# A tile of 56 words behind the constants of a convolution and feed-forward kernel on one core

## Chip, core and metric

The kernel runs on one core of one Trainium2 chip. The metric is the device time of one execution in microseconds, lower is better. Engines are named as in the profile: PE is TensorE's matmul, PEld its weight load, DVE VectorE, ACT ScalarE, POOL GpSimd, SP SyncE.

## What is computed

A long convolution by FFT, gated by its input, and then a feed-forward layer with silu on every token. B = 2, S = 12,480, D = 128, d_ff = 2,048.

```python
h_filt = (np.maximum(pos_emb @ w1, 0.0) @ w2) * np.exp(-0.01 * pos)[:, None]
u = x * v
y = irfft(rfft(u, 2 * S) * rfft(h_filt, 2 * S))[:, :S]
t = (x * y).reshape(B * S, D)
h = t @ w_in
out = (h / (1.0 + np.exp(-h))) @ w_out
```

## The kernel before, in words

The transform of 2 x 98 x 64 points is done as matmuls with tables of sines in two stages. Five stretches follow each other in the program, and the order in each is written out by hand (strings of letters, and tables of offsets).

1. To some 125 us: products x * v, stage A of batch 0 (L224, into X), the filter's first layers (zp, z) and their stage A (aph, into Xha and Xhb). The feed-forward weights, which arrive as 64-bit floats, are made fp32 beside it.
2. To some 300 us, a loop of 49 pairs of frequencies for batch 0: filter spectrum (hp, sp, hab), forward transform (up, L437), complex product (at, bt), inverse transform (wp, L437), store (ws, L492). The table fb is loaded four pairs ahead, hab is stored to DRAM for batch 1. These matmuls are plain fp32.
3. To some 400 us: stage A of batch 1, and the split of w_in and w_out.
4. To some 957 us: the feed-forward steps of batch 0, and between them, by a table of offsets, the same loop for batch 1 (up and wp, now in fp32r), whose loads and temporaries lie in the buffer slots.
5. To the end: the remaining feed-forward steps alone.

A feed-forward step (L838 to L877) treats 512 tokens and one of 16 blocks of 128 hidden units. Accuracy is kept in fp32r by splitting each operand into a high and a low part and multiplying three times. So a step has three matmuls of 512 columns into hq, with weights from wih and wil and the moving operand ah and al (L845 to L847), and, three steps later, three into op, with weights from woh and wol and the moving operand gh and gl (L875 to L877). The silu (L852), the split into gh and gl (L854 to L857), the last inverse transform of the next tokens (yp, L620) and its split (ah, al, L642) go on beside. There are 49 x 16 = 784 steps; up and wp of batch 1 have 2 x 49 x 6 = 588 matmuls of 256 columns (L437).

Buffers are taken from two sides of SBUF. On the left, from the constants upwards: X, z, and in their turn fb, zt, hab, uw, at, bt, ws, then woh, wol, ring, ah, al, gh, gl, ot, g and the split operands of up and wp (xs, fw, iv, vs with h and l). On the right, from the top downwards: the staged x and v, the weights' temporaries, Xha, Xhb, then slots, wih, wil and spare. In the built program the first left buffer behind the constants, X, starts at byte 20,480 of each partition; woh at 120,832, wol at 129,024, ah at 141,312, gh at 149,504: all left buffers from X on start at multiples of 512. On the right wih starts at 187,360, wil at 195,552, slots at 203,744: 32 bytes short of a multiple of 512.

Of the kernel before, what the change touches and what calls it, by code (L numbers as in the profile page):

```python
# [10 lines left out]
F32 = mybir.dt.float32  # L11
# [83 lines left out]
def kernel(  # L95
# [20 lines left out]
    def pool(name, **kw):  # L116
        kw.setdefault("bufs", 1)
        return tc.alloc_tile_pool(name=name, reuse_waits="tile", **kw)
# [8 lines left out]
    const = pool("const")  # L127
# [4 lines left out]
    win_sb = const.tile([R, 128], F32, name="win_sb")  # L132
    w1_sb = const.tile([128, 128], F32, name="w1_sb")
    w2_sb = const.tile([128, D], F32, name="w2_sb")

    def weights(wp, src, nm, bufs, dst):

# [834 lines left out]
```

## Time and profile before

| | us |
|---|---|
| median of 3 runs (lowest, highest) | 1614.35 (1613.84, 1619.06) |
| profiled execution | 1615.36 |
| its span, first to last instruction | 1613.6 |
| busy: PE, DVE, ACT, POOL | 1582.2, 1234.4, 1058.5, 566.3 |

TensorE's granted clock is 0.993 of full speed over the span. Busy times of matmuls are of limited use, since they are pipelined: one of 512 columns is shown with about 0.39 us, and the next starts 0.23 us after it. Start times in the timeline are therefore read beside the means. The chain of waits follows the work that ended last back to the start, and the table by stages tells which engine has no idle time where.

### The profile page before, as it was taken

How to read it: one execution, taken by the hardware profiler on the slowest of the kernel's cores; microseconds unless marked ns; L12 is line 12 of the kernel's file. 1: busy time of each engine (PE TensorE's matmuls, PEld its weight loads, DVE VectorE, ACT ScalarE, POOL GpSimd, SP SyncE). 2: the span in 40 equal slices, each digit the busy share in tenths (PEclk: the TensorE clock that was granted, in tenths of full speed). 3: DMA queues.
4: the chain of work that ended last, by engine and by line, in shares of the span. 5: the costliest groups of instructions: out<-in, count | busy, mean ns of one | idle time of the engine just before them, and what ended most of it. 6: DMA issues, size and time to landing. Idle time of an engine off the chain costs nothing.

```text
span 1613.6 us, 29344 instructions
## 1 busy us (share of the span) xinstructions
PE 1582.2 (98%) x10904; PEld 1316.2 (82%) x10904; DVE 1234.4 (77%) x1983; ACT 1058.5 (66%) x1929; POOL 566.3 (35%) x564
## 2 busy tenths in 40 slices
PE   7799999899999999999999999999999999999999
PEld 7797877688888888888888888888888888888887
DVE  5946888755688988889988887777777777777776
ACT  4548888687777777777777765555555555555554
POOL 4627779532266666666666630000000000000000
PEclk9899999899999999999999999999999999999999
DMA  8817888834355454455545521111111211111100
GB/s 256 244 62 210 235 248 250 235 115 119 91 145 149 130 140 129 132 140 137 149 132 141 145 78 47 48 33 45 51 32 45 66 33 45 51 32 45 51 28 14
DMA packets 125767, 180.75 MB, mean 112 GB/s; under 512 B 10528, under 2 KB 72360, under 8 KB 125624
## 3 DMA queue, kind: packets, MB, share of 16 engines
q1 hardware_dynamic: 85560, 141.14, 31.7%
q10 hardware_dynamic: 40064, 37.73, 8.1%
q8 instruction: 86, 1.41, 0.4%
q14 instruction: 57, 0.47, 0.1%
HBM read 125.42 MB, written 53.41 MB: 111 GB/s over the span
## 4 chain that ended last, share of the span: by engine, by line
PE 92%; DMA 4%; DVE 2%; POOL 1%; issue 1%; ACT 0%; SPq 0%; ACTq 0%; POOLq 0%; DVEq 0%
PE op L875 12%; PE hq L846 11%; PE hq L845 11%; PE op L877 11%; PE hq L847 11%; PE op L876 11%; PE yp L620 6%; PE wp L437 4%; PE up L437 4%; PE ap L224 3%; PE sp L316 2%; PE aph L358 2%; PE hp L297 2%; DMA xs<-in_x_dram 2%; DMA fb<-in_fb_dram 1%
## 5 line engine op out<-in xcount | busy, mean ns | idle before, releaser
L852 ACT ACTIVATE g<-hq 128x512 f32<-128x512 f32 x424 | 253.8, 599 | 238.8 <-PE hq L847 227.9
L857 DVE TENSOR_TENSOR gl<-g,gh 128x512 fp32r<-128x512 f32 x424 | 293.6, 693 | 99.1 <-ACT gh L856 66.4
L875 PE MATMUL op<-gh,woh 128*128 128x512 f32 (+1 forms) x784 | 313.8, 400 | 0.0
L845 PE MATMUL hq<-ah,wih 128*128 128x512 f32 (+1 forms) x784 | 309.2, 394 | 0.9 <-DVE gl L857 0.8
L846 PE MATMUL hq<-al,wih 128*128 128x512 f32 (+1 forms) x784 | 309.7, 395 | 0.0
L877 PE MATMUL op<-gh,wol 128*128 128x512 f32 (+1 forms) x784 | 308.7, 394 | 0.0
L847 PE MATMUL hq<-ah,wil 128*128 128x512 f32 (+1 forms) x784 | 308.2, 393 | 0.0
L876 PE MATMUL op<-gl,woh 128*128 128x512 f32 (+1 forms) x784 | 305.7, 390 | 0.0
L852 ACT ACTIVATE hq<-hq 128x512 f32<-128x512 f32 (+1 forms) x360 | 206.7, 577 | 101.6 <-PE hq L847 85.0
L857 DVE TENSOR_TENSOR gl<-hq,gh 128x512 fp32r<-128x512 f32 (+1 forms) x360 | 244.7, 684 | 33.3 <-ACT gh L856 23.3
L854 DVE CAST gh<-hq 128x512 fp32r<-128x512 f32 (+1 forms) x270 | 183.3, 679 | 54.8 <-ACT hq L852 53.0
L854 DVE CAST gh<-g 128x512 fp32r<-128x512 f32 x318 | 135.7, 427 | 66.4 <-ACT g L852 65.2
L847 PEld LDWEIGHTS hq<-ah,wil 128*128 128x128 f32 x784 | 146.9, 187 | 35.5
L846 PEld LDWEIGHTS hq<-al,wih 128*128 128x128 f32 x784 | 146.9, 187 | 34.8 <-DVE al L643 0.2
L875 PEld LDWEIGHTS op<-gh,woh 128*128 128x128 f32 x784 | 147.6, 188 | 33.5
L845 PEld LDWEIGHTS hq<-ah,wih 128*128 128x128 f32 x784 | 147.4, 188 | 32.9 <-DVE gl L857 1.6
L877 PEld LDWEIGHTS op<-gh,wol 128*128 128x128 f32 x784 | 147.1, 188 | 31.4
L876 PEld LDWEIGHTS op<-gl,woh 128*128 128x128 f32 x784 | 147.7, 188 | 27.5 <-DVE gl L857 0.3
L230 ACT COPY X<-ap 64x392 f32<-64x392 f32 x208 | 100.0, 481 | 39.4 <-PE ap L224 36.8
L620 PEld LDWEIGHTS yp<-fai_sb,slots 98*64 98x64 f32 x2048 | 89.3, 138 | 19.2 <-issue 18.7
L620 PE MATMUL yp<-fai_sb,slots 98*64 98x97 f32 (+1 forms) x2048 | 99.3, 251 | 0.0
L475 DVE TENSOR_TENSOR at<-at,bt 128x768 f32<-128x768 f32 x49 | 72.5, 1479 | 19.5 <-POOL bt L469 19.0
(1059 smaller groups left out, 2400.5 us busy)
## 6 DMA issues: line engine op xcount, KB each, us to landing
slots<-hs SPq DMA_DIRECT2D x98, 256.0 KB
slots<-wd SPq DMA_DIRECT2D x48, 490.0 KB
hs<-hab SPq DMA_DIRECT2D x49, 256.0 KB
wd<-ws SPq DMA_DIRECT2D x49, 256.0 KB
slots<-in_fb_dram SPq DMA_DIRECT2D x49, 256.0 KB
wd<-slots ACTq DMA_DIRECT2D x49, 256.0 KB
out_dram<-ot ACTq DMA_DIRECT2D x48, 256.0 KB
fb<-in_fb_dram ACTq DMA_DIRECT2D x45, 256.0 KB
```

The costliest lines, as they stand in the source:

```text
L230: nc.scalar.copy(out=o, in_=src[:, k0:k1])
L437: nc.tensor.matmul(out[:, k].rearrange("p i d -> p (i d)"), f[:, k], a[:, k], start=(i == 0), stop=(i == len(passes) - 1),)
L620: nc.tensor.matmul(yp[h : h + 64, o : o + ws[t]], wt[:, c, t * D + h : t * D + h + 64], fai_sb[:, c, 0 : ws[t]], start=(c == 0), stop=(c = ...
L845: nc.tensor.matmul(hp[:, 0:w], wih[:, fs], ah[:, 0:w], start=True, stop=False)
L846: nc.tensor.matmul(hp[:, 0:w], wih[:, fs], al[:, 0:w], start=False, stop=False)
L847: nc.tensor.matmul(hp[:, 0:w], wil[:, fs], ah[:, 0:w], start=False, stop=True)
L852: nc.scalar.activation(out=g[:, 0:w], in_=hp[:, 0:w], func=AF.Silu)
L854: nc.vector.tensor_copy(gh[:, 0:w], g[:, 0:w])
L857: nc.vector.tensor_tensor(out=gl[:, 0:w], in0=g[:, 0:w], in1=gh[:, 0:w].bitcast(F32), op=ALU.subtract)
L875: nc.tensor.matmul(o[:, 0:w], woh[:, fs], gh[:, 0:w], start=(f == 0), stop=False)
L876: nc.tensor.matmul(o[:, 0:w], woh[:, fs], gl[:, 0:w], start=False, stop=False)
L877: nc.tensor.matmul(o[:, 0:w], wol[:, fs], gh[:, 0:w], start=False, stop=(f == NF - 1))
```

## The change

One tile is taken from the pool of the constants, behind w2_sb. Nothing writes or reads it. It has 56 words of 4 bytes, so X and every left buffer behind it start 224 bytes higher: X at 20,704, woh at 121,056, gh at 149,728. The constants ahead of it and all buffers on the right stay where they are, and so does PSUM. On every engine and queue the instructions stand in the same order with the same shapes and waits as before.

```diff
     win_sb = const.tile([R, 128], F32, name="win_sb")
     w1_sb = const.tile([128, 128], F32, name="w1_sb")
     w2_sb = const.tile([128, D], F32, name="w2_sb")
+    const.tile([128, 56], F32, name="gap")
```

## Rows read from the trace of the kernel before

**Rows 1.** The page's chain that ended last, by line.

```profile
PE op L875 12%; PE hq L846 11%; PE hq L845 11%; PE op L877 11%; PE hq L847 11%; PE op L876 11%; PE yp L620 6%; PE wp L437 4%; PE up L437 4%; PE ap L224 3%; PE sp L316 2%; PE aph L358 2%; PE hp L297 2%; DMA xs<-in_x_dram 2%; DMA fb<-in_fb_dram 1%
```

**Rows 2.** Stages: length, busy us (count) of PE, PEld, DVE, ACT, POOL; clock, DMA, GB/s.

```profile
125.00:300.00 175.00, 169.23 (x2158) 135.72 (x2159) 142.76 (x204) 143.41 (x258) 141.83 (x148) 1.00 0.84 235
...
400.00:957.00 557.00, 556.96 (x3351) 464.81 (x3350) 484.42 (x744) 420.55 (x800) 336.49 (x347) 1.00 0.50 134
957.00:1613.00 656.00, 652.98 (x3646) 528.37 (x3644) 470.85 (x821) 356.21 (x592) 0.00 (x0) 1.00 0.14 42
```

**Rows 3.** Timeline of TensorE, 1290 to 1297 us: start us, length us, what.

```profile
1290.30 0.39 PE L875 MATMUL op<-gh,woh 128*128 128x512 f32 x1
...
1290.75 0.40 PE L877 MATMUL op<-gh,wol 128*128 128x512 f32 x1
...
1291.45 0.39 PE L847 MATMUL hq<-ah,wil 128*128 128x512 f32 x1
...
1295.84 0.39 PE L875 MATMUL op<-gh,woh 128*128 128x512 f32 x1
```

**Rows 4.** Groups by line and shape, 1289.5 to 1306.5 us: busy us, mean ns | idle.

```profile
L846 PE MATMUL hq<-al,wih 128*128 128x512 f32 x13 | 5.2, 397 | 0.0
L877 PE MATMUL op<-gh,wol 128*128 128x512 f32 x13 | 5.1, 396 | 0.0
L845 PE MATMUL hq<-ah,wih 128*128 128x512 f32 x13 | 5.1, 394 | 0.0
L876 PE MATMUL op<-gl,woh 128*128 128x512 f32 x13 | 5.1, 389 | 0.0
L847 PE MATMUL hq<-ah,wil 128*128 128x512 f32 x12 | 4.7, 393 | 0.0
L875 PE MATMUL op<-gh,woh 128*128 128x512 f32 x12 | 4.7, 389 | 0.0
...
L847 PEld LDWEIGHTS hq<-ah,wil 128*128 128x128 f32 x13 | 2.4, 187 | 0.6
L875 PEld LDWEIGHTS op<-gh,woh 128*128 128x128 f32 x12 | 2.3, 188 | 0.6
```

**Rows 5.** The page's costliest groups: the silu of each step, without and with side work.

```profile
L852 ACT ACTIVATE g<-hq 128x512 f32<-128x512 f32 x424 | 253.8, 599 | 238.8 <-PE hq L847 227.9
...
L852 ACT ACTIVATE hq<-hq 128x512 f32<-128x512 f32 (+1 forms) x360 | 206.7, 577 | 101.6 <-PE hq L847 85.0
```

**Rows 6.** Groups by line and shape, 700 to 712 us, beside batch 1.

```profile
L847 PE MATMUL hq<-ah,wil 128*128 128x512 f32 x8 | 3.2, 396 | 0.0
L845 PE MATMUL hq<-ah,wih 128*128 128x512 f32 x8 | 3.2, 395 | 0.0
L846 PE MATMUL hq<-al,wih 128*128 128x512 f32 x8 | 3.2, 395 | 0.0
L875 PE MATMUL op<-gh,woh 128*128 128x512 f32 x8 | 3.1, 394 | 0.0
L877 PE MATMUL op<-gh,wol 128*128 128x512 f32 x8 | 3.1, 393 | 0.0
L876 PE MATMUL op<-gl,woh 128*128 128x512 f32 x8 | 3.1, 393 | 0.0
```

**Rows 7.** Timeline of TensorE at 707 us, two of six 256-column matmuls.

```profile
707.68 0.28 PE L437 MATMUL up<-xs26l,fw26h 128*128 128x256 f32 x1
707.80 0.28 PE L437 MATMUL up<-xs26h,fw26l 128*128 128x256 f32 x1
```

**Rows 8.** Groups by line and shape, whole span.

```profile
L437 PE MATMUL wp<-at,fb 128*128 128x256 f32 x196 | 51.1, 383 | 3.5 <-POOL at L479 2.6 <-DVE at L479 0.9
...
L491 ACT COPY slots<-wp 128x512 f32<-128x512 f32 x49 | 28.8, 588 | 0.3
L491 ACT COPY ws<-wp 128x512 f32<-128x512 f32 x49 | 28.7, 586 | 14.7 <-ACT hab L318 9.5 <-PE wp L437 3.8 <-issue 1.2
```

**Rows 9.** Chain of waits, 140 to 300 us, by line.

```profile
by line: PE sp L316 21.3%; PE wp L437 19.9%; PE up L437 17.8%; PE hp L297 14.6%; DMA fb<-in_fb_dram 12.5%; DVE at L475 3.6%; issue 2.9%; POOL bt L462 2.3%; POOL bt L469 1.9%; ACT hab L318 0.9%; POOL at L479 0.9%; ACT ws L491 0.4%; ACT uw L4
```

## Prediction

> **What bounds the kernel now.** I read the chain of waits first. By line, the six matmul lines of the feed-forward step (L845 to L847, L875 to L877) hold 67% of it [rows 1]. The busy time by stage says where: in 400 to 957 us TensorE is busy 556.96 of 557 us, in 957 to 1613 us 652.98 of 656 us, while VectorE has 470.85 and ScalarE 356.21 there [rows 2]. So for three quarters of the run a nanosecond per matmul counts at full weight, and a nanosecond on any other engine counts nothing.
>
> Then I looked at those matmuls one by one. Where the side work is over, one step (six matmuls of 512 columns) takes (1295.84 - 1290.30) / 4 = 1.385 us [rows 3]. The six are alike in shape, type and source of the moving operand (left side of SBUF). They are not alike in time. A weight load runs beside the matmul before it, so each matmul is to be read by whose weights load in its shadow. 875, 876 and 847 cover loads of woh, wol and woh, from the left side: 389, 389 and 393 ns. 877, 845 and 846 cover loads of wih, wih and wil, from the right side: 396, 394 and 397 ns. Means 390.3 and 395.7, so **5.3 ns more beside a load from the right** [rows 4]. The start times say the same: 875 to 877 takes 0.45 us for two matmuls, 877 to 847 takes 0.70 us for three [rows 3]. The loads themselves last 187 or 188 ns on both sides [rows 4]. In the built program the left buffers from X on start at multiples of 512 bytes, the right ones 32 bytes short of one. The change puts the left ones at 224 past a multiple of 256, which is where the right ones already stand (256 - 32). That 5.3 ns is what I build on.
>
> **The change part by part.** No instruction, wait or transfer is added, removed or reordered; the unused tile is never written. What differs is the address of every left buffer.
>
> *Weights on the left, steps without side work.* If a load from 224 past a multiple costs what the right side costs now, three matmuls in each of the 424 steps that write g [rows 5] take 5.3 ns more: 424 x 3 x 5.3 = 6.7 us.
>
> *Weights on the left, steps beside batch 1.* Here the six lines are level: 394, 393 and 396 ns beside left loads, 393, 395 and 395 beside right ones [rows 6]. The same classes exist, but the 256-column matmuls between the steps disturb the pattern. If everything goes to the 395.7 of the undisturbed right class, that is 1.4 ns on the six matmuls of 360 steps [rows 5]: 3.0 us. The low end is 0, the high end the whole 5.3 on the three left loads, 5.7 us. I take 3.0, as it starts from this stretch's own rows.
>
> *The 256-column matmuls of up and wp in batch 1.* 2 x 49 x 6 = 588, all with left weights and 0.12 us apart [rows 7]. At 5.3 ns each: 3.1 us; low end 0. I take 3.1, because they have no right neighbours that could have hidden the price already.
>
> *The moving operand.* All 4,704 + 588 of these matmuls stream from the left, so all streams now begin at 224. No row has an fp32r stream from there. Lower bound: a gain, which is the second rival below. Upper bound: another 5.3 ns each, 5,292 x 5.3 = 28.0 us. I take 0, since what the rows vary is the weight side alone, and keep both ends.
>
> *Matmuls in plain fp32 (batch 0, stage A, yp).* They run as two slower passes: 383 ns for 256 columns [rows 8], against 0.28 us for the fp32r form [rows 7]. A stream at that pace has more slack for a late word, so I take 0. At the high end each pays 5.3 ns on 383, 1.4% of the 73.6% of 160 us that sp, wp, up and hp hold on the chain of the batch 0 loop [rows 9]: 1.6 us.
>
> *The other engines.* The same ScalarE eviction takes 588 ns into a right buffer and 586 into a left one [rows 8]. Two nanoseconds per instruction lie under the busy TensorE; if that cover were gone, the 784 silus and 98 evictions like these would cost 1.8 us. VectorE and GpSimd have slack in the same stages [rows 2]. I take 0.
>
> *DMA.* In the batch 0 loop fb, hab and ws are on the left; in batch 1 the same kinds of transfer use the slots on the right. Share of the queues per GB/s: 0.84 / 235 = 0.00357 with left buffers, 0.50 / 134 = 0.00373 with right ones, 4.4% more [rows 2]. The chain of that loop waits for landings of fb for 12.5% of 160 us, 20 us [rows 9]; 4.4% of that is 0.9 us, low end 0. I take 0: the queues go from 0.84 to 0.88 busy and the prefetch is four ahead.
>
> The Trainium skill's page "DMA: Bandwidth & Descriptors" (How a descriptor splits into AXI transactions) speaks against the change: a read that does not start on a multiple of 256 bytes still fetches from the boundary below. By it a 512-byte run of ws would take 23 beats instead of 16, an estimate of 44% on a third of the loop's bytes, so some 15% on those waits, 3 us instead of 0. The 4.4% above, which includes the same 512-byte runs stored from the right, does not bear out so much.
>
> **Sum.** 6.7 + 3.0 + 3.1 = 12.8 us. The profiled execution took 1615.36 us, so 1628.2; the median of the runs, 1614.35, lies 1.0 lower, so **1627 us**. Bounds of this case alone: 1621 (the first term, the others at 0) to 1662 (every high end, 47.8 us).
>
> **The rivals.** *Nothing happens.* The 5.3 ns could belong to where wih and wil lie (at 187 KB of a partition, the left weights at 121 to 137 KB), or to the hq bank they feed, and 224 bytes alter neither. For it: ScalarE is blind to the side within 2 ns [rows 8], and all six lines are level in the stage with side work [rows 6]. Against: 875 to 877 and 845 to 847 differ in little else that repeats. Time: 1614.
>
> The Trainium skill's page "SBUF — State Buffer" would have it so: TensorE has separate read ports for weights and stream and waits for nobody (Who interferes with whom), and its line is 16 bytes, of which 224 is a whole number. By that rule the sum is 0. The trace shows 389 and 397 ns for equal work [rows 4], which the rule leaves unexplained.
>
> *It becomes faster.* The 5.3 ns may not be a price of standing at 224, but of weights and stream standing differently. After the change stream, left weights and right weights all stand 32 bytes below a multiple of 256, and the right loads would cost what the left ones do now. Price: in 424 steps 3 x 5.3 ns, 6.7 us; beside batch 1 all six from 394.3 to 389, 360 x 6 x 5.3 = 11.4 us; together 18.1, so 1596 us; 1608 if only the first holds. For it: beside batch 1 left loads stand at 393 to 396 ns [rows 6], so the time also depends on what went before and not on the address alone. Against: it needs misplaced reads to do no harm at all. It decides at one place: whether 877, 845 and 846 fall to 389 ns, or 875 and 876 rise to 396.
>
> *Streams pay too.* Each of the 5,292 matmuls reads one more piece than before: 28.0 us more, 1655 us. It is the upper part of my own case, and it is decided by the step: 1.385 us now, 1.40 in my sum, 1.43 here.
>
> **How the numbers follow.** Under 0.3% (4.8 us) a measurement of this kernel cannot tell a change from none. Slower, by weights alone or with streams: 0.43, of which a quarter for the streams. Nothing: 0.24, the addresses being the likelier reading of the two classes. Faster: 0.33, since the equal standing of all buffers is as exact as the misplacement. The likeliest is the first, with its own range of 1621 to 1662. Since faster holds a third, the whole range has to reach down to its full price: 1595 to 1652, which leaves out the top of the streams' case and the chance that more than one term is wrong.
>
> **What would show it.** In the profile after: 875, 876 and 847 at 394 to 397 ns between two yp tiles, and a step of about 1.40 us; the 256-column matmuls over 0.12 us apart; weight loads still 187 to 188 ns; the side pair of ScalarE unchanged; the loop before 300 us at its old length. Wrong if the step stays 1.385 us (nothing), falls to about 1.37 (equal standing), or if the loss sits before 300 us with more waits for fb (DMA).

## The result: 1.1% faster, and the profile after

The changed kernel takes **1596.41 us** (median of 4 runs, 1595.97 to 1599.0) against 1614.09 (4 runs) before on the same chip: ratio 0.989, 95% interval 0.9878 to 0.9903. The forecast was slower. The profiled execution took 1596.24 us, its span 1594.5, at a granted clock of 0.992. One of the ten runs of e5 below took 2221 us at a granted clock of 0.654, and ratios leave such a run out.

The chain by line after (before: [rows 1]); all lines behind the new tile have moved down by one:

```profile
PE op L876 12%; PE op L877 11%; PE hq L846 11%; PE op L878 11%; PE hq L847 11%; PE hq L848 11%; PE yp L621 6%; PE up L438 5%; PE wp L438 4%; PE sp L317 3%; PE ap L225 3%; PE aph L359 2%; PE hp L298 2%; DMA xs<-in_x_dram 1%; DVE X L233 1%
```

The same six lines bound the kernel. The stages, columns as in [rows 2]:

```profile
125.00:300.00 175.00, 170.04 (x2136) 136.34 (x2134) 144.46 (x204) 144.19 (x261) 145.85 (x149) 1.00 0.83 237
400.00:950.00 550.00, 549.89 (x3349) 464.56 (x3348) 483.32 (x744) 418.54 (x798) 335.60 (x347) 1.00 0.50 135
950.00:1594.00 644.00, 640.84 (x3641) 527.90 (x3639) 468.71 (x819) 355.82 (x591) 0.00 (x0) 1.00 0.15 43
```

TensorE has next to no idle time, as before (3.2 of 644 us in the last stage, against 3.0 of 656), and the clock is the same 1.00 (its level of 2.4 GHz): it does the same work in less time. Two starts of the first hq matmul, five steps apart, after and before:

```profile
1300.85 0.39 PE L846 MATMUL hq<-ah,wih 128*128 128x512 f32 x1
...
1307.65 0.39 PE L846 MATMUL hq<-ah,wih 128*128 128x512 f32 x1
```

```profile
1295.14 0.39 PE L845 MATMUL hq<-ah,wih 128*128 128x512 f32 x1
...
1302.08 0.39 PE L845 MATMUL hq<-ah,wih 128*128 128x512 f32 x1
```

A step fell from 1.387 to **1.360 us**. I count steps in slots of 6.667 ns (16 cycles at 2.4 GHz), since most steps of both traces are whole numbers of them. A step has 208 slots before and 204 after, 34 for each matmul. All six lines now stand level, 1296 to 1312 us (before: [rows 4]):

```profile
L847 PE MATMUL hq<-al,wih 128*128 128x512 f32 x13 | 5.1, 389 | 0.0
L876 PE MATMUL op<-gh,woh 128*128 128x512 f32 x12 | 4.7, 390 | 0.0
L878 PE MATMUL op<-gh,wol 128*128 128x512 f32 x12 | 4.7, 390 | 0.0
L848 PE MATMUL hq<-ah,wil 128*128 128x512 f32 x12 | 4.7, 389 | 0.0
L846 PE MATMUL hq<-ah,wih 128*128 128x512 f32 x12 | 4.7, 389 | 0.0
L877 PE MATMUL op<-gl,woh 128*128 128x512 f32 x12 | 4.7, 389 | 0.0
```

Beside batch 1, 700 to 712 us, they went from 393 to 396 ns [rows 6] to 390 to 392:

```profile
L877 PE MATMUL op<-gl,woh 128*128 128x512 f32 x7 | 2.7, 392 | 0.0
...
L846 PE MATMUL hq<-ah,wih 128*128 128x512 f32 x6 | 2.3, 390 | 0.0
```

Laying the starts of the same instruction in both traces beside each other tells where the 19.1 us between the two spans went: 2.3 us by the end of the batch 0 loop (1.9 of them before 100 us), 1.6 in all at 398 us, 7.9 at 945, 19.1 at the end. So 6.3 us came beside batch 1 and 11.2 in the steps alone. They agree with 424 steps x 26.7 ns = 11.3. The 1.9 us at the start are not the change's: e4 below, a kernel with no gain, is 2.2 us ahead at 100 us too, and two executions of one program (e12, e16) differ by 5.5 us there.

### The profile page after: what moved, and what is told of

Its sections match the earlier page's. It is cut to its first block, busy times and chain, and to the rows that moved or that the text cites. A ratio compares the mean times of both kernels' runs of the same rounds, so it can differ in the third digit from the quotient of the medians.

```text
span 1594.5 us, 29344 instructions
## 1 busy us (share of the span) xinstructions
PE 1560.7 (98%) x10904; PEld 1314.0 (82%) x10904; DVE 1231.1 (77%) x1983; ACT 1057.4 (66%) x1929; POOL 566.3 (36%) x564
## 4 chain that ended last, share of the span: by engine, by line
PE 91%; DMA 4%; DVE 2%; POOL 1%; issue 1%; ACT 1%; SPq 0%; ACTq 0%; POOLq 0%; DVEq 0%
PE op L876 12%; PE op L877 11%; PE hq L846 11%; PE op L878 11%; PE hq L847 11%; PE hq L848 11%; PE yp L621 6%; PE up L438 5%; PE wp L438 4%; PE sp L317 3%; PE ap L225 3%; PE aph L359 2%; PE hp L298 2%; DMA xs<-in_x_dram 1%; DVE X L233 1%
## 5 line engine op out<-in xcount | busy, mean ns | idle before, releaser
L846 PE MATMUL hq<-ah,wih 128*128 128x512 f32 (+1 forms) x784 | 306.0, 390 | 0.1
L847 PE MATMUL hq<-al,wih 128*128 128x512 f32 (+1 forms) x784 | 305.0, 389 | 0.0
L848 PE MATMUL hq<-ah,wil 128*128 128x512 f32 (+1 forms) x784 | 304.8, 389 | 0.0
L878 PE MATMUL op<-gh,wol 128*128 128x512 f32 (+1 forms) x784 | 304.8, 389 | 0.0
L878 PEld LDWEIGHTS op<-gh,wol 128*128 128x128 f32 x784 | 147.2, 188 | 30.6
```

Of the source, the lines that this page charges most:

```text
L846: nc.tensor.matmul(hp[:, 0:w], wih[:, fs], ah[:, 0:w], start=True, stop=False)
L847: nc.tensor.matmul(hp[:, 0:w], wih[:, fs], al[:, 0:w], start=False, stop=False)
L848: nc.tensor.matmul(hp[:, 0:w], wil[:, fs], ah[:, 0:w], start=False, stop=True)
L878: nc.tensor.matmul(o[:, 0:w], wol[:, fs], gh[:, 0:w], start=False, stop=(f == NF - 1))
```

## Experiments

In the expectations, theory 1 is that the distance between weights and stream counts, theory 2 that the place of a buffer does. All places below are bytes of a partition modulo 256. Each edit is to the kernel before unless said otherwise. Steps are measured from the start of one first hq matmul to the next, over the steps of the last stage that no yp interrupts; in slots, mean of some 400. Each ratio is to runs of the kernel before that were taken beside that kernel.

| kernel | woh, wol | wih, wil | ah, al | gh, gl | slots per step | us, ratio with interval |
|---|---|---|---|---|---|---|
| before | 0 | 224 | 0 | 0 | 208.0 | 1614.09 |
| after | 224 | 224 | 224 | 224 | 204.2 | 1596.41, 0.989 (0.9878 to 0.9903) |
| e1 | 0 | 224 | 224 | 224 | 208.1 | 1613.2, 0.9989 (0.998 to 0.9999) |
| e2 | 0 | 0 | 0 | 0 | 204.2 | 1595.05, 0.9881 (0.9864 to 0.9898) |
| e3 | 32 | 224 | 32 | 32 | 208.7 | 1614.88, 1.0002 (0.999 to 1.0013) |
| e4 | 0 | 224 | 0 | 0 | 208.0 | 1614.9, 1.0003 (0.9991 to 1.0016) |
| e5 | 0 | 224 | 224 | 0 | 209.0 | 1616.59, 1.0008 (0.999 to 1.0027) |
| e6 | 96 | 224 | 96 | 96 | 208.6 | 1615.41, one run |
| e7 | 192 | 224 | 192 | 192 | 208.1 | 1611.93, one run |
| e8 | 224 | 224 | 224 | 224 | 204.2 | 1594.44, one run |
| e9 | 224 | 224 | 0 | 0 | 210.0 | 1621.03, 1.0048 (1.0033 to 1.0063) |
| e10 | 224 | 224 | 224 | 0 | 208.1 | 1614.51, 1.0 (0.9987 to 1.0013) |
| e11 | 0, 224 | 0, 224 | 0 | 0 | 208.2 | 1615.73, 1.0007 (0.9994 to 1.002) |
| e12 | 224 | 240 | 224 | 224 | 209 or 204 | 1604.99, one run |

**e1 to e4: place or distance?** e1 moves the streams alone (the tile goes behind woh and wol), e2 the right buffers alone (its pool is released at the end, not shown), e3 and e4 change the size of the tile.

```diff
e1           mt = pool("mt")
+            mt.tile([128, 56], F32, name="gap")
e2   ...
+    gap_pool = pool("gap_pool", side="right")
+    gap_pool.tile([128, 120], F32, name="gap")
     stg = pool("stg", side="right")
e3  +    const.tile([128, 8], F32, name="gap")
e4  +    const.tile([128, 64], F32, name="gap")
```

> The tile of 56 words lies behind woh and wol instead of behind the constants, so that only ring, ah, al, gh, gl, ot, g and the split operands of up and wp start at 224; woh and wol stay at a multiple of 512. Theory 1 (the distance between the weights that are loaded and the stream that runs meanwhile counts): matmuls that cover loads of wih and wil fall to 389 ns, those that cover woh and wol rise to 394 to 397; the step stays near 1.385 us and the time near 1614, 1606 to 1618. Theory 2 (a stream that starts at 224 is good by itself, whatever the weights): all six at 389, step 1.360, time near 1597.

> The left side as before; a tile of 120 words at the top of the right side moves every right buffer down by 480 bytes, so that wih, wil and slots start at multiples of 512, as the left buffers do. Theory 1 (distance): all six matmuls at 389 ns, step 1.360, time 1594 to 1599. Theory 2 (a stream from 224 is good): nothing changes for the streams, step 1.385, time near 1614.

> 8 words behind the constants instead of 56: left buffers at 32, right ones at 224 (both counted from a multiple of 256). Distance of 192 bytes. If the distance counts by lines of 64 bytes, it is 0 there: step 1.360, time 1594 to 1599. If it counts by 256 bytes, a price of its own, between 389 and 397 ns beside right loads, and 389 beside left ones: time 1597 to 1620.

> 64 words behind the constants: left buffers move by 256 bytes. If distances count by 256 bytes or less, all is as before: 394 to 397 ns beside right loads, step 1.385, time near 1614. If they count by 512, another price, between 1597 and 1620.

e2 leaves every left buffer where it was and gains 1.2%, as much as the change within the intervals: no price belongs to the place 224 itself. Its first hq matmul, five steps apart, has the step of 1.360 us:

```profile
1297.45 0.39 PE L847 MATMUL hq<-ah,wih 128*128 128x512 f32 x1
...
1304.25 0.39 PE L847 MATMUL hq<-ah,wih 128*128 128x512 f32 x1
```

e4 moves the left side by 256 and changes nothing, so what counts repeats at 256 bytes. The changed kernel says the same: its left buffers stand at 224 and its right ones at 480 past a multiple of 512, and nothing is paid. e3, at a distance of 192, rules out 64. e1 turns the classes around. Its groups, 1297 to 1306 us:

```profile
L847 PE MATMUL hq<-al,wih 128*128 128x512 f32 x7 | 2.8, 393 | 0.0
L848 PE MATMUL hq<-ah,wil 128*128 128x512 f32 x7 | 2.7, 393 | 0.0
L846 PE MATMUL hq<-ah,wih 128*128 128x512 f32 x7 | 2.7, 387 | 0.0
L876 PE MATMUL op<-gh,woh 128*128 128x512 f32 x6 | 2.4, 397 | 0.0
L878 PE MATMUL op<-gh,wol 128*128 128x512 f32 x6 | 2.4, 397 | 0.0
L877 PE MATMUL op<-gl,woh 128*128 128x512 f32 x6 | 2.4, 395 | 0.0
```

With the weights where they were, op is now the slower half (395 to 397), hq (stream and weights both at 224) the faster (387 to 393). Here theory 1 missed: by it the third op matmul (L878), which covers a load of wih, should have fallen to 389, and it stands at 397. So the load beside a matmul does not decide alone.

**e5 to e8: pairs, and other distances.** e5 puts ah and al at the place of wih and wil, and leaves gh, gl, woh, wol at 0. e6 to e8 change the tile to 24, 48, 52 words.

```diff
e5       ring.append(mt.tile([128, 2 * WM], F32, name="ring"))
+        mt.tile([128, 56], F32, name="gap")
     moe = pool("moe")
+    moe.tile([128, 8], F32, name="gap2")
```

> Weights woh, wol and streams gh, gl stand at 0 mod 256, weights wih, wil and streams ah, al at 224: within each matmul stream and weights stand alike, but the loads that run beside the third op matmul (wih beside gh) and beside the third hq matmul (woh beside ah) stand 224 apart from the running stream. Theory A (a matmul pays for the distance between its own weights and its stream): step 1.360 us, 204 slots of 6.667 ns, 1595 to 1598 us. Theory B (a running stream pays for the distance of the load beside it): two of six pay, step 1.375 to 1.380 us, 1604 to 1610 us. If one place for all buffers were needed, whatever the pairs: step 1.387 us, 1614 us.

> Left buffers at 96 mod 256, right ones at 224: distance 128. If only the place modulo 128 counts: step 1.360 us, 1596 us. If the place modulo 256 counts: step 1.387 us, 1614 us.

> Left buffers at 192, right ones at 224: distance 32. If any distance costs the same: step 1.387 us, 1614 us. If the price grows with the distance (224 costs 26.7 ns per step): step 1.364 us, 1598 us, or, measured the shorter way round as 32 of 128, the same 26.7 ns as before.

> Left buffers at 208, right ones at 224: distance 16. If any distance costs the same: step 1.387 us, 1614 us. If the price grows with the distance: step 1.360 to 1.375 us, 1596 to 1606 us.

e5 refutes both A and B: 209 slots, though each matmul has its stream where its weights are. Its third case, one place for all buffers, came nearest. Two starts, five steps apart:

```profile
1234.78 0.39 PE L847 MATMUL hq<-ah,wih 128*128 128x512 f32 x1
...
1241.75 0.40 PE L847 MATMUL hq<-ah,wih 128*128 128x512 f32 x1
```

e6 rules out a period of 128; e7 pays in full for a distance of 32. e8 was a miss: tiles take a multiple of 32 bytes, so 52 words put the left side at 224, not 208. It is the changed kernel again, and gives its step again.

After e5 all cases fitted one more idea, theory W: only the weights have to stand alike.

**e9 to e12: weights among themselves?** e9 and e10 are the changed kernel with 8 words more ahead of all streams, or of gh and gl alone. e11 has 56 words between woh and wol and between wih and wil, and 8 ahead of the streams (edit not shown). e12 is the changed kernel with wih and wil read 16 bytes further on.

```diff
e9       mt = pool("mt")
+        mt.tile([128, 8], F32, name="gap")
e10  moe = pool("moe")
+    moe.tile([128, 8], F32, name="gap2")
e12
-    wi_split[:] = (mwi.tile([128, DFF], F32R, name=f"wi{t}") for t in "hl")
+    wi_split[:] = (mwi.tile([128, DFF + 64], F32R, name=f"wi{t}")[:, 4 : 4 + DFF] for t in "hl")
```

> All four weight buffers at 224 mod 256, all streams (ah, al, gh, gl, split operands) at 0. Theory W (what counts is that the weights of consecutive loads stand alike; the stream's place is free): step 1.360 us, 1595 to 1599 us. Theory S (distance between weights and stream, own or beside): all six matmuls pay, step 1.400 us or more, 1620 to 1640 us.

> All four weight buffers and the streams ah, al at 224 mod 256, the streams gh, gl at 0. Theory W: step 1.360 us, 1595 to 1599 us. Theory S: op pays as hq does before, step 1.387 us, 1614 us. If a change of the stream's place from one matmul to the next costs: two changes per step, step 1.387 us, 1614 us.

> woh and wih at 0 mod 256, wol and wil at 224, streams at 0: the place of the weights changes four times per step instead of two. Theory W, two slots of 6.667 ns per change: 8 slots over 204, step 1.413 us, 784 x 26.7 ns = 21 us over before, 1632 to 1636 us. Theory S, by pairs: two of six matmuls (those with wol and wil) pay 9 ns each, step 1.378 us, 1607 us.

> As the changed kernel, but wih and wil are read from 16 bytes further on (240 mod 256, woh and wol at 224): a distance of 16 between the weights, half of the 32 that cost 26.7 ns per step. If any distance costs the same: step 1.387 us, 1614 us. If 16 bytes are within tolerance: step 1.360 us, 1596 us.

e9 refutes W, and bears theory S out: with all four weights alike and all streams 32 bytes away, a matmul takes 35 slots in the mean instead of 34, and of e1 to e12 this is the only kernel measurably slower than before. Two starts, five steps apart:

```profile
1237.80 0.40 PE L847 MATMUL hq<-ah,wih 128*128 128x512 f32 x1
...
1244.80 0.39 PE L847 MATMUL hq<-ah,wih 128*128 128x512 f32 x1
```

But S as a price per pair fails at e11. Call a matmul's stream and its own weights its pair. In e11 two pairs of six are apart, as are two of the loads beside, and it costs the 4 slots that three pairs cost in e10 and before. Theory W's 8 slots did not come either. One rival is argued against but not taken out by any run: that TensorE's reads meet those and the writes of other engines. Against it speaks that e12 moves only weights that TensorE alone reads in the last stage, and still has steps of 209 slots. And the difference is there too beside batch 1, where the other engines do other work: undisturbed steps have medians of 208.2 slots before and 205.5 after.

**Two scans: the price over the distance.** Both edit the changed kernel (one run each, 1620.72 and 1619.48 us, beside 1615.70 before). The streams get buffers of 576 words and are read from an offset that changes with the tile, here one of the 49 blocks of 512 tokens; the weights stay at 224.

```diff
-        ah = mt.tile([128, WM], F32R, name=f"ah{n}", tag="ah", bufs=2)
+        ah = mt.tile([128, WM + 64], F32R, name=f"ah{n}", tag="ah", bufs=2)[:, off(n, 0) : off(n, 0) + WM]
...
-            gl = moe.tile([128, 512], F32R, name=f"gl{s}", tag="gl", bufs=P['lag'] + 1)
+            gl = moe.tile([128, 576], F32R, name=f"gl{s}", tag="gl", bufs=P['lag'])[:, off(n, 3) : off(n, 3) + 512]
```

> As the changed kernel, but in tiles 23 to 48, which run without batch 1, all four streams are read from an offset of 0, 1, 2, 3, 4, 6, 8, 10, 12, 14, 16, 20, 24, 28, 32, 36, 40, 44, 48, 52, 56, 58, 60, 62, 63, 0 words (one value a tile) inside buffers of 576 words; the weights stay at 224 mod 256; gl has one buffer less, ot too. Theory S (distance of a stream from the weights modulo 64 words): 204 slots per step (1.360 us) at 0 words, 210 (1.400 us) at 8 and near it, as with the streams 8 words (32 bytes) above the weights; the values between are open; 206 to 207 at 4 words. Theory D (any distance over some words costs the same): 204 at 0 only and 210 everywhere else.

> As the scan of common offsets, but with offsets of 8, 16, 24, 32, 40, 48, 56 words (one a tile) first on gh and gl alone (tiles 23 to 29), then on al and gl alone (30 to 36), then on ah and al alone (37 to 43), then four mixtures and 0. Theory S, a price per pair of a matmul's own stream and weights: gh and gl alone, or ah and al alone, cost half of what all four cost (three of six matmuls), al and gl alone a third (two of six). Theory L (all of a step must keep one phase, or it is lost for all): any of them costs 4 to 6 slots.

Steady slots per step with all streams at one offset (two values: it switched within the tile):

```
words  0   1   2   3   4     6   8   10  12      14  16  20  24
slots  204 213 210 206 208.5 210 210 210 207/210 207 206 208 210
words  28  32  36  40  44  48  52      56  58  60  62      63
slots  208 209 210 211 210 210 211/207 210 210 213 207/210 204
```

Five steps at 1 word, and at 0 words in the last tile:

```profile
1020.54 0.40 PE L851 MATMUL hq<-ah,wih 128*128 128x512 f32 x1
...
1027.64 0.40 PE L851 MATMUL hq<-ah,wih 128*128 128x512 f32 x1
...
1603.45 0.39 PE L851 MATMUL hq<-ah,wih 128*128 128x512 f32 x1
...
1610.25 0.39 PE L851 MATMUL hq<-ah,wih 128*128 128x512 f32 x1
```

One word off costs most, as do 60: 1.420 us a step. Only 0 and one word below it (63) give 204. Over these 256 bytes the price follows no slope, and neither S (206 to 207 slots at 4 words) nor D (210 everywhere else) came true. In the second scan, offsets on gh and gl alone cost 3 to 6 slots, on ah and al alone 3 to 6, on al and gl alone (two matmuls of six) 2 to 6, and mixtures 3 to 6: not half and a third of what all six cost. At 16 words gh and gl alone even cost 5.5, where all four streams cost 2. So no fixed price per pair fits. Theory L, a step that loses as a whole, fits better, a little wider than its 4 to 6; more is not shown for it. None of the 50 placements is under 204.

**Does the distance alone decide?** e12 had steps of 209 slots up to tile 35, of 204 to tile 47, then 209 again. e15 scans with every second tile at 0; e16 is e12 once more.

> Scan of the streams' offset, weights at 224 mod 256, but every second tile from 23 on at 0 words, and between them 2, 3, 4, 8, 16, 32, 48, 56, 60, 61, 62, 63 words, so that each is entered from a stretch at 204 slots. Theory P (the distance alone sets the step): each offset has the step of the first scan (2 words 210, 3 words 206, 8 words 210, 16 words 206, 32 words 209, 48 words 210, 56 words 210, 63 words 204), and the tiles at 0 return to 204 each time. Theory H (several steps are stable at one distance, and the one before or a disturbance picks): some offsets keep 204 or settle at another value than in the first scan.

> The kernel with wih and wil 16 bytes on, again: in its first run it did steps of 209 slots up to tile 35, of 204 to tile 47, and 209 again, and took 1605 us. Theory P: 1605 us each time, with the change at the same tiles. Theory H: the executions differ by how many steps run at 204, from 1596 us (all at 204) to 1618 us (all at 209), and in the profiled one the change sits elsewhere or does not come.

The repeat switched at the same steps of tiles 35 and 47. Two stretches of it, tiles 33 and 40:

```profile
1237.89 0.40 PE L846 MATMUL hq<-ah,wih 128*128 128x512 f32 x1
...
1244.86 0.40 PE L846 MATMUL hq<-ah,wih 128*128 128x512 f32 x1
...
1407.26 0.39 PE L846 MATMUL hq<-ah,wih 128*128 128x512 f32 x1
...
1414.06 0.39 PE L846 MATMUL hq<-ah,wih 128*128 128x512 f32 x1
```

1.393 and 1.360 us, same code, same addresses. It switches at the yp matmuls of a tile, and the same way in both profiled executions. In e15 all 13 tiles at 0 came back to 204 after at most five steps; 2, 3, 4, 8, 32, 48, 56 and 63 words took the steady values of the first scan, 16 words stood at 210 until yp and at 206 after it, 60 words at 210 and 213, 61 words at 216 (the most seen) and 210. So theory H holds at a distance (several steady steps, yp picks one), and at distance 0 only 204 was seen. H was wrong in that the profiled execution would pick differently. That one took 1613.29 us, but it lies 8.3 behind e12's by 500 us (5.5 of them by 72 us) and no more after it. The 10 runs of e16 took 1605.51 to 1614.9 us (ratio 0.9969, 0.9954 to 0.9983); what steps the other nine had is not shown.

## Why the prediction was wrong

*What bounds the kernel* was right: six lines, next to no idle time, and the gain came from nanoseconds per matmul.

*The two classes* were read as left loads against right loads. The split was real, its cause not: e1 swaps the classes without moving a weight, e2 removes them without moving a left one. Busy times also hid part of it: by starts (medians of the last stage), 845 to 847 and 877 are 231 to 235 ns apart from the next matmul, 875 and 876 226.7, so four of six paid, 26.7 ns a step and not 3 x 5.3.

***Weights on the left, steps without side work* is the step that failed.** It tied the price to an address, 224 past a multiple, where it belongs to a difference of addresses: with streams and weights all at one place the price is gone. It said +6.7 us; it was -11.2. The step of 1.400 us that the sum expected exists, in e9: weights at 224, streams left at 0. There the whole came to +7.4 us (1621.03 against 1613.64).

*Beside batch 1* and *the 256-column matmuls*: +3.0 and +3.1 forecast, together -6.3 measured. The up and wp matmuls had stream and weights alike before and have so after, and start 18 slots (0.12 us) apart most often in both; in the mean 119.9 and 120.0 ns, so nothing was paid there.

*The moving operand* was set to 0 with both ends kept open. It is half of the matter: where it stands against the weights is what counts (e9 against the changed kernel, 210 slots against 204).

*Plain fp32* at 0 was right: in the batch 0 loop sp's weights moved by 224 bytes against its moving operand, and it stayed at 275 ns. *Other engines* at 0 was right: the pair of [rows 8] is now 587 and 585.

```profile
L317 PE MATMUL sp<-w_sb,zt 64*64 64x128 f32 x1568 | 54.3, 275 | 0.2 <-ACT X L231 0.2
...
L492 ACT COPY slots<-wp 128x512 f32<-128x512 f32 x49 | 28.8, 587 | 0.3
L492 ACT COPY ws<-wp 128x512 f32<-128x512 f32 x49 | 28.7, 585 | 14.3 <-ACT hab L319 9.9 <-issue 2.6 <-PE wp L438 1.7
```

*DMA* at 0 was right: after the change it is 0.83 of the queues for 237 GB/s, no more per byte than the 0.84 for 235 of [rows 2], and waits for fb hold 5.1% of the chain from 140 to 300 us, against 12.5% [rows 9]. The 3 us estimated beside it did not come.

*The rivals.* "It becomes faster" gave the mechanism, the sign and 1596 us. That its total came out so near is luck: its parts were 6.7 in the steps alone and 11.4 beside batch 1, measured 11.2 and 6.3. The place that was to decide did: 877, 845 and 846 fell to 389 or 390. Beside "Nothing" stood the Trainium skill, page "SBUF — State Buffer" (Who interferes with whom), by which TensorE waits for nobody. The sum of 0 drawn from it is not what was measured: places alone are worth 4 slots a step. Nor does a whole number of 16-byte lines keep the step short: an offset of 4 words, 16 bytes, costs 4.5 slots in the scan.

The chances were wrong in one place: equal standing was called "as exact as the misplacement" and still put behind it. The trace of before had a sign of it: 875 and 876, with stream and weights alike, were the fast ones, and 877, with both alike but a load of wih beside it, was not.

## What to carry to other kernels

When alike matmuls differ in time, list for each the place of its stream, of its weights and of the load beside it, and look at differences of places before blaming one of them. For fp32r matmuls back to back, put all streams and all weights of a loop at one place modulo 256 bytes; an unused tile of the right size on either side does it, and here it gave 1.1 to 1.2%. Read steps from starts, not from busy times.

## What was not expected of the hardware

Equal fp32r matmuls of 512 columns took 204 to 216 slots of 6.667 ns per six in steady stretches, with nothing changed but places in SBUF. Two misplaced matmuls can cost as much as three (e11, e10). One distance can have two steady steps, and the two executions profiled (e12, e16) took the same one at each step of the last stage. What in the chip makes the places meet is not shown: these runs tell the period of 256 bytes, the tolerance of one word below, and that plain fp32 (sp) is untouched.
